# k of batches 1 to 7 transposed by the DMA crossbar instead of TensorE, in a fused two-layer attention and token-mixing kernel

## The chip, the cores and the metric

One NeuronCore of a Trainium2 chip. The metric is device time in microseconds (us) for one execution. Executions of one kernel differ: those of the kernel before took 126.76 to 129.70 us. A run over 1.5% above the fastest of the same kernel is called slow, and ratios use the fast runs alone. "The profile" below is one traced execution; its span runs from the first to the last instruction and is about 1.8 us shorter than the device time.

## The reference, cut to what matters

```python
# q, k, v: [8 batches, 8 heads, 576, 64] float32;  p: [8, 8, 32, 64]
def sm_attn(qq, kk, vv):                       # softmax(q k^T / 8) v
    s = scale * np.matmul(qq, kk.transpose(0, 1, 3, 2)); ...
p_packed = sm_attn(p, k, v)                    # 32 packed rows per head
x = sm_attn(q, p_packed, p_packed)             # back to 576 rows
wq, wk = x @ w_q, x @ w_k                      # token mixing, no softmax
mixed  = (wq @ wk^T / 8) @ x
out    = relu(mixed) @ w_out                   # [8, 576, 512] float32
```

The change concerns the first product only, p against k: in this kernel's matmuls the axis that is summed over lies on the partitions (the rows of on-chip memory), so k has to lie with its 64 head columns on partitions. It arrives with rows on partitions and is transposed: 18 blocks of 128x128 per batch.

## The kernel before

A hand-ordered list names every step; each engine runs its steps strictly in that order. A step `KT.b.c` transposes some of batch b's k blocks on TensorE into PSUM (the memory that TensorE writes), `KE.b.c@V` (or `@A`) copies them to SBUF (the main on-chip memory) on VectorE (or ScalarE), `S1.b.c` multiplies them with p, `X1` takes the exponential. Loads `LD.*` of batches 1 to 7 are issued by GpSimd, stores (inside `OE`) by SyncE (SP).

```python
inpool = ...bufs=4      # k and q as loaded (bf16)      epool = ...bufs=2   # kT and others
opool  = ...bufs=5      # output tiles waiting for their stores
...
def load(x):
    ...
    elif a == "k":
        t = k_in[b] = inpool.tile([P, 2 * C, W], bf16, tag="k_sb", name="k_sb")
        nc.gpsimd.dma_start(t, rows(k, b))          # 576 KB in SBUF, float32 -> bf16 on the way
...
def KT(b, c, eng, bk):                              # 18 blocks in three groups of 8, 8 and 2
    ...
    for n, m in enumerate(ms):
        nc.tensor.transpose(ps[:, n], src[:, m * P:(m + 1) * P], idb if b else idf)
def KE(b, c, eng, bk):
    copy(eng, new("kT", b, [P, NZ, P], pool=epool)[:, z0:z1], T["kt", b, c])
def S1(b, c, eng, bk):                              # scores: needs kT
    ...
    nc.tensor.matmul(ps[...], T["kT", b][:, place(b, m), halves(i)], rhs, start=True, stop=True)
...
def OE(b, t, eng, bk):                              # after every second output tile:
    ...
    for s in range(4):
        nc.sync.dma_start(dst[:, s * 1024:(s + 1) * 1024], o[s * GQ:(s + 1) * GQ]...)
```

A piece of the order, around batch 2:

```
OE.0.2@V WKQ.1.2=0 SET.g2@V OE.0.1@A WE.1.0@V KT.2.1=4 WR.1.0@V WE.1.1@A WR.1.1@V KT.2.2=1
KE.2.1@V GM.1=3 GE.1.1@V LD.q3 GE.1.0@A KT.2.0=5 Y.1=2 KE.2.2@V KE.2.0@V RLR.0@V YE.1@A S1.2.1=7
```

The softmax here doesn't subtract the row's maximum and nothing guards it: scores larger than these inputs give would overflow.

## Time and profile before

| | before |
|---|---|
| device time, median of 2 runs | 128.91 us (128.38 to 129.43) |
| span of the profile, mean granted TensorE clock | 127.6 us, 0.967 |
| TensorE / VectorE / ScalarE busy | 84% / 69% / 62% |
| issue to landing of a k load, median | 19.5 us |

From the page of the kernel before: the span; the busy time of the engines; three rows of 40 equal slices, each digit the busy share in tenths (PEclk: granted clock in tenths); the engines' shares of the chain of work that ended last; and three groups of instructions (engine, operation, output and inputs, shapes, count, busy us, mean ns, idle time before them and who ended it).

```profile
span 127.6 us, 4277 instructions
PE 106.7 (84%) x1794; PEld 71.7 (56%) x1794; DVE 87.9 (69%) x231; ACT 79.0 (62%) x168; POOL 34.6 (27%) x49
...
PE   0299793899998899879999999996999999989800
...
PEclk9999999657999999999999999999999999999997
DMA  3999999399999999999999999999995002664893
...
PE 62%; DVE 11%; ACT 9%; DMA 5%; issue 5%; POOL 3%; SPq 1%; POOLq 0%; ACTq 0%; DVEq 0%
...
L134 ACT ACTIVATE kT<-kT_ps 128x256 bf16<-128x256 bf16 (+2 forms) x8 | 4.8, 595 | 8.7 <-PE kT_ps L286 8.7
...
L138 DVE COPY kT<-kT_ps 128x1024 bf16<-128x1024 bf16 (+1 forms) x15 | 8.8, 606 | 1.2 <-PE kT_ps L286 1.0
L286 PE MATMUL kT_ps<-idb,k_sb 128*128 128x128 bf16 x126 | 9.4, 220 | 0.0
```

TensorE is busy nearly everywhere and holds most of the chain, and the DMA row says 9 tenths until late. The 126 bf16 transposes (L286) overlap one another, so 9.4 us of busy time is an upper bound of what they cost.

The timeline of the kernel before around batch 2 (start, duration, engine, line, operation), cut to SP's stores and to the way of k to the scores:

```profile
38.29 3.83 SPq L521 DMA_DIRECT2D out_dram<-o  x8
...
39.54 0.72 PE L286 MATMUL kT_ps<-idb,k_sb 128*128 128x128 bf16 x10
40.38 0.69 DVE L138 COPY kT<-kT_ps 128x1024 bf16<-128x1024 bf16 x1
...
40.46 0.61 PE L286 MATMUL kT_ps<-idb,k_sb 128*128 128x128 bf16 x8
41.43 0.89 DVE L138 COPY kT<-kT_ps 128x256 bf16<-128x256 bf16 x2
...
41.97 0.44 PE L305 MATMUL e_ps<-pdiag,kT 128*64 128x64 bf16 x16
```

From the first transpose to the first score matmul takes 2.4 us: the transposes hold TensorE for about 1.0 us of it, and the rest is other matmuls and a wait of 0.7 us for ScalarE. SP has issued the last store of this group only at 42.1, when the scores already start.

### The profile page before, as it was taken

What the parts mean: (1) busy time and instruction counts of PE and PEld (TensorE: products, weight loads), DVE (VectorE), ACT (ScalarE), POOL (GpSimd) and SP (SyncE); (2) the same over time, 40 slices, a digit from 0 to 9 for tenths busy, and PEclk for the clock granted to TensorE, in tenths of its full rate; (3) what the DMA queues carried; (4) which work ended last, traced back from release to release, by engine and by line L of the source; (5) the groups of instructions that cost most, each with busy time, mean ns of one, the idle gap of its engine ahead of it and who ended that gap; (6) DMA issues with size and microseconds to landing.
All of it is one profiled execution on the core that took longest, in us unless ns stands there. A gap on an engine that the chain in (4) does not pass through costs nothing.

```text
span 127.6 us, 4277 instructions
## 1 busy us (share of the span) xinstructions
PE 106.7 (84%) x1794; PEld 71.7 (56%) x1794; DVE 87.9 (69%) x231; ACT 79.0 (62%) x168; POOL 34.6 (27%) x49
## 2 busy tenths in 40 slices
PE   0299793899998899879999999996999999989800
PEld 0285382677647447658747764874587765544300
DVE  3028899644996835878998898687785999926310
ACT  4003423962975763977966688785889898578300
POOL 7800211990097000195029004100305006000000
PEclk9999999657999999999999999999999999999997
DMA  3999999399999999999999999999995002664893
GB/s 43 358 201 210 197 206 213 58 161 139 204 212 207 285 285 253 306 255 212 208 208 212 284 283 211 238 309 266 217 251 149 1 5 85 164 167 121 234 285 105
DMA packets 16292, 25.55 MB, mean 200 GB/s; under 512 B 2904, under 2 KB 11096, under 8 KB 16272
## 3 DMA queue, kind: packets, MB, share of 16 engines
q0 software_dynamic: 10720, 14.32, 64.3%
q1 hardware_dynamic: 5552, 10.95, 28.4%
q8 instruction: 14, 0.23, 0.7%
q14 instruction: 6, 0.05, 0.1%
HBM read 30.15 MB, written 9.44 MB: 310 GB/s over the span
## 4 chain that ended last, share of the span: by engine, by line
PE 62%; DVE 11%; ACT 9%; DMA 5%; issue 5%; POOL 3%; SPq 1%; POOLq 0%; ACTq 0%; DVEq 0%
PE out_ps L505 18%; PE kT_ps L286 7%; PE pv_ps L323 5%; PE qT_ps L364 5%; PE aT_ps L415 4%; DMA k<-in_k_dram 3%; PE e_ps L383 3%; POOL a L406 3%; PE e_ps L305 3%; PE mix_ps L475 3%; PE warm_ps L542 2%; DVE rs L395 2%; PE wkq_ps L435 2%; ACT e L311 2%; ACT e L389 2%
## 5 line engine op out<-in xcount | busy, mean ns | idle before, releaser
L505 PE MATMUL out_ps<-wout,relu 128*128 128x512 bf16 x128 | 30.5, 379 | 1.0 <-DVE rec L328 1.0
L406 POOL TENSOR_TENSOR a<-e,rr 128x512 bf16<-128x512 f32 (+1 forms) x15 | 14.0, 947 | 61.5 <-DVE rr L400 39.9
L134 ACT ACTIVATE o<-out_ps 128x512 f32<-128x512 f32 x26 | 15.5, 598 | 8.1 <-PE out_ps L505 7.9
L505 PEld LDWEIGHTS <-relu 128*128 128x128 bf16 x128 | 11.5, 98 | 14.1 <-issue 2.1
L395 DVE TENSOR_REDUCE rs<-e 128x16 f32<-128x512 f32 (+1 forms) x24 | 13.9, 579 | 2.3 <-ACT e L389 2.3
L311 ACT ACTIVATE e<-e_ps 128x512 bf16<-128x512 f32 (+1 forms) x24 | 11.0, 492 | 3.7 <-PE e_ps L305 3.4
L389 ACT ACTIVATE e<-e_ps 128x512 f32<-128x512 f32 (+1 forms) x24 | 12.0, 528 | 1.8 <-PE e_ps L383 1.8
L487 DVE TENSOR_SCALAR relu<-mix_ps 128x512 bf16<-128x512 f32 x17 | 11.0, 683 | 0.0
L364 PE MATMUL qT_ps<-idb,q_sb 128*64 128x128 bf16 x288 | 10.8, 221 | 0.0
L138 DVE COPY qT<-qT_ps 128x1024 bf16<-128x1024 bf16 (+1 forms) x16 | 8.9, 584 | 2.6 <-PE qT_ps L364 2.5
L134 ACT ACTIVATE kT<-kT_ps 128x256 bf16<-128x256 bf16 (+2 forms) x8 | 4.8, 595 | 8.7 <-PE kT_ps L286 8.7
L323 PE MATMUL pv_ps<-v_sb,e 64*64 64x192 bf16 x288 | 9.0, 262 | 0.9 <-ACT e L311 0.9
L138 DVE COPY kT<-kT_ps 128x1024 bf16<-128x1024 bf16 (+1 forms) x15 | 8.8, 606 | 1.2 <-PE kT_ps L286 1.0
L286 PE MATMUL kT_ps<-idb,k_sb 128*128 128x128 bf16 x126 | 9.4, 220 | 0.0
L364 PEld LDWEIGHTS <-q_sb 128*64 128x64 bf16 x288 | 8.6, 110 | 1.1 <-issue 0.4
L305 PE MATMUL e_ps<-pdiag,kT 128*64 128x64 bf16 x288 | 8.2, 203 | 1.1 <-ACT kT L134 0.8
L415 PE MATMUL aT_ps<-idb,a 128*128 128x128 bf16 x80 | 7.9, 231 | 1.3 <-POOL a L406 0.7
L286 PE MATMUL kT_ps<-idf,k 128*128 128x128 f32 x18 | 4.3, 425 | 5.5 <-DMA k<-in_k_dram 5.5
L485 ACT ACTIVATE relu<-mix_ps 128x512 bf16<-128x512 f32 x15 | 8.3, 599 | 0.6 <-PE mix_ps L475 0.5
L305 PEld LDWEIGHTS <-kT 128*64 128x64 bf16 x288 | 6.6, 117 | 3.6 <-issue 1.2
L323 PEld LDWEIGHTS <-e 64*64 64x64 bf16 x288 | 6.4, 113 | 3.4 <-issue 1.3
L138 DVE COPY o<-out_ps 128x512 f32<-128x512 f32 x6 | 4.1, 688 | 5.8 <-PE out_ps L505 5.8
(79 smaller groups left out, 197.7 us busy)
## 6 DMA issues: line engine op xcount, KB each, us to landing
out_dram<-o SPq DMA_DIRECT2D x64, 128.0 KB, 4.2
v_sb<-in_v_dram POOLq DMA_DIRECT2D x8, 576.0 KB, 18.8
q_sb<-in_q_dram POOLq DMA_DIRECT2D x8, 576.0 KB, 17.8
k_sb<-in_k_dram POOLq DMA_DIRECT2D x7, 576.0 KB, 19.5
k<-in_k_dram SPq DMA_DIRECT2D x2, 576.0 KB, 4.8
out_dram<-o_rem SPq DMA_DIRECT2D x4, 256.0 KB, 4.3
wout<-in_moe_w_out_dram POOLq DMA_DIRECT2D x2, 256.0 KB, 4.1
pbf<-in_p_dram POOLq DMA_DIRECT2D x1, 224.0 KB, 11.7
```

Of the source, the lines that this page charges most:

```text
L134: nc.scalar.activation(o, i, COPY)
L138: nc.vector.tensor_copy(o, i)
L286: nc.tensor.transpose(ps[:, n], src[:, m * P:(m + 1) * P], idb if b else idf)
L305: nc.tensor.matmul(ps[halves(i), at[0]:at[1] + 1:at[1] - at[0]], T["kT", b][:, place(b, m), halves(i)], rhs, start=True, stop=True)
L311: nc.scalar.activation(e1[:, 2 * z0:2 * z1], T["s1", b, c], EXP, scale=scale)
L323: nc.tensor.matmul(T["pv", b][i][halves(cc)], lhsT, rhs, start=n == 0, stop=n == R - 1, skip_group_check=True)
L364: nc.tensor.transpose(ps[halves(x), z - z0], q_in[b][:, x, r * Dh:(r + 1) * Dh], idb)
L389: nc.scalar.activation(e2, T["s2", b, c].rearrange("a t i c (x l) -> a (t i c x) l", l=L), EXP, scale=scale)
L395: nc.vector.tensor_reduce(rs, T["e2", (b, c)], axis=AX, op=ADD)
L406: e.tensor_tensor(a2[:, 2 * c:2 * c + n].rearrange("a t i (u l) -> a (t i u) l", l=L), T["e2", (b, c)], T["rr", (b, c)].to_broadcast((P, n ...
L415: nc.tensor.transpose(ps[:, i, t - 2 * c], T["a2", b][:, t, i], idb)
L505: nc.tensor.matmul(ps, lhsT, wout[:, j, :], start=j == 0, stop=j == NJ - 1)
```

## The change

Intent: free TensorE of 126 transposes and VectorE and ScalarE of 21 copies out of PSUM, by one DMA transpose per batch (a crossbar transpose), SBUF to SBUF, issued by SP. Every `KT.b.*` and `KE.b.*` of batches 1 to 7 leaves the order, and one `TR.b` stands where the batch's first `KT` stood:

```diff
-OE.0.2@V WKQ.1.2=0 SET.g2@V OE.0.1@A WE.1.0@V KT.2.1=4 WR.1.0@V WE.1.1@A WR.1.1@V KT.2.2=1
-KE.2.1@V GM.1=3 GE.1.1@V LD.q3 GE.1.0@A KT.2.0=5 Y.1=2 KE.2.2@V KE.2.0@V RLR.0@V YE.1@A S1.2.1=7
+...OE.0.1@A WE.1.0@V TR.2 WR.1.0@V WE.1.1@A WR.1.1@V GM.1=3 GE.1.1@V LD.q3 GE.1.0@A Y.1=2 RLR.0@V
+YE.1@A S1.2.1=7 ...                       (the same for batches 1 and 3 to 7)
@@
     def place(b, m):
-        return sum(KM if b else KM0, []).index(m)
+        return m if b else sum(KM0, []).index(m)
@@
+    def TR(b, eng, bk):
+        kT = new("kT", b, [P, NZ, P], pool=epool)
+        nc.sync.dma_start(kT, k_in[b].rearrange("a u n -> a (u n)"), transpose=True)
```

More of the change, by code (lines that the diff above doesn't have):

```diff
@@ L16 @@
 WC.0@P PP.0.0@V QE.0.2@A PT.0=7 PE.0@A QE.0.1@V PX.1=1 S2.0.1=3 QE.0.0@V WC.1@P PXE.1.0@V S2.0.0=2
-PXE.1.1@V X2.0.1@A S2.0.2=4 X2.0.0@A RS.0.1@V PX.2=0 KT.1.2=5 RR.0.1@V PXE.2.1@A AM.0.1@P QK.0=7
-RS.0.0@V KT.1.0=6 X2.0.2@A KT.1.1=3 RR.0.0@V AM.0.0@P RS.0.2@V KE.1.2@A AT.0.1=1 RR.0.2@V AM.0.2@V
-AT.0.2=2 PXE.2.0@A KE.1.0@A S1.1.2=4 X1.1.2@A LD.O LD.k2 AT.0.0=5 KE.1.1@V AE.0.2@A AE.0.1@V
-S1.1.0=0 QKE.0@A X1.1.0@A S1.1.1=3 WKQ.0.2=6 X1.1.1@A WKQ.0.1=4 WR.0.0@A AE.0.0@V WKQ.0.0=1
-WE.0.1@V PV.1.0=2,5 WR.0.1@V LD.v2 WE.0.0@A SET.g0@V PV.1.1 PV.1.2 RC.1.1@V RC.1.0@V GM.0=7
@@ L22 @@
-PP.1.0@V PP.1.1@V GE.0.0@V QT.1.1=0 GE.0.1@A PT.1=3 Y.0=4 QT.1.0=6 YE.0@V QT.1.2=1 PE.1@V QE.1.1@A
-LD.q2 QE.1.0@V MX.0.0=2,5 MX.0.1=7,4 S2.1.1=3 QE.1.2@A S2.1.2=0 S2.1.0=1 LD.k3 MR.0=6 RL.0.0@A
-RL.0.1@A QK.1=2 RL.0.2@V RL.0.3@V X2.1.2@A X2.1.0@A RS.1.2@V RR.1.2@V RS.1.0@V RR.1.0@V LD.v3
-X2.1.1@A OT.0.3=5 RS.1.1@V OT.0.0=7 OE.0.3@A AM.1.2@P RR.1.1@V AM.1.0@P OT.0.2=0 QKE.1@A AT.1.0=4
-OE.0.0@A AM.1.1@V AT.1.2=1 AE.1.0@A AE.1.2@A AT.1.1=3 OT.0.1=5 WKQ.1.0=2 AE.1.1@A WKQ.1.1=7
-OE.0.2@V WKQ.1.2=0 SET.g2@V OE.0.1@A WE.1.0@V KT.2.1=4 WR.1.0@V WE.1.1@A WR.1.1@V KT.2.2=1
@@ L28 @@
-KE.2.1@V GM.1=3 GE.1.1@V LD.q3 GE.1.0@A KT.2.0=5 Y.1=2 KE.2.2@V KE.2.0@V RLR.0@V YE.1@A S1.2.1=7
-MR.1=0 MX.1.0=4,3 RLR.1@V X1.2.1@A MX.1.1=1,2 S1.2.0=5 OT.1.4=6 RL.1.2@V RL.1.3@A RL.1.0@A
-RL.1.1@V OT.1.0=7 OT.1.1=0 LD.k4 LD.v4 OE.1.4@A OT.1.2=3 OE.1.0@A X1.2.0@A OT.1.3=2 PV.2.0=4,1
-S1.2.2=6 OE.1.2@A LD.q4 OE.1.1@V SET.v3@V OE.1.3@A X1.2.2@A QT.2.2=7 PV.2.1 PV.2.2 QE.2.2@V
-KT.3.2=5 RC.2.1@V QT.2.1=0 QT.2.0=3 RC.2.0@V PP.2.1@V QE.2.0@A PP.2.0@V PT.2=2 QE.2.1@V PE.2@V
-KT.3.0=6 S2.2.2=7 S2.2.1=1 X2.2.2@A KE.3.0@V KE.3.2@V S1.3.0=4 QK.2=0 S1.3.2=2 X2.2.1@A RS.2.2@V
@@ L34 @@
-RS.2.1@V S2.2.0=3 X1.3.0@A X2.2.0@A KT.3.1=7 KE.3.1@A PV.3.0=6,5 RR.2.1@V X1.3.2@A S1.3.1=1 LD.k5
-RR.2.2@V RS.2.0@V QKE.2@A RR.2.0@V AM.2.2@P AM.2.1@P AM.2.0@V LD.v5 AT.2.1=4 X1.3.1@A AT.2.2=3
-AT.2.0=7 PV.3.1 AE.2.0@A AE.2.2@V PV.3.2 AE.2.1@V LD.q5 WKQ.2.2=2 WKQ.2.1=0 WKQ.2.0=1 WR.2.0@A
-RC.3.1@V PP.3.1@V RC.3.0@V QT.3.1=3 WR.2.1@A PP.3.0@V WE.2.0@A QT.3.2=4 WE.2.1@V GM.2=7 QE.3.2@A
-GE.2.1@A QE.3.1@V PT.3=5 QT.3.0=2 PE.3@V GE.2.0@V LD.k6 Y.2=6 S2.3.2=0 S2.3.1=1 KT.4.0=4 KT.4.2=3
-QE.3.0@A YE.2@V X2.3.2@A KE.4.2@A KT.4.1=5 KE.4.0@V LD.v6 MX.2.1=7,6 X2.3.1@A MX.2.0=2,0 S1.4.0=3
@@ L40 @@
-S1.4.2=4 QK.3=1 KE.4.1@V RL.2.0@V LD.q6 S1.4.1=5 S2.3.0=2 RL.2.1@V RL.2.3@A RL.2.2@V X1.4.0@A
-RS.3.1@V X1.4.1@A RR.3.1@V PV.4.0=6,3 X1.4.2@A X2.3.0@A RS.3.2@V RR.3.2@V PV.4.1 PV.4.2 RC.4.0@V
-OT.2.1=7 PP.4.0@V AM.3.2@P OT.2.3=5 OE.2.1@A RS.3.0@V QKE.3@A OE.2.3@A RR.3.0@V OT.2.2=4 AT.3.2=0
-OT.2.0=2 AM.3.1@V RC.4.1@V AM.3.0@P AE.3.2@V WKQ.3.2=7 MR.2=6 OE.2.2@A PP.4.1@V AT.3.1=1 PT.4=5
-AE.3.1@V OE.2.0@A AT.3.0=4 AE.3.0@V KT.5.0=0 WKQ.3.1=3 RLR.2@A PE.4@A LD.k7 WKQ.3.0=2 LD.v7
-QT.4.1=1 WE.3.0@A KE.5.0@V WE.3.1@V WR.3.1@V LD.q7 S1.5.0=6 WR.3.0@A GM.3=5 KT.5.1=4 KT.5.2=0
@@ L46 @@
-QE.4.1@V GE.3.1@A GE.3.0@V KE.5.2@A Y.3=3 X1.5.0@A YE.3@A KE.5.1@V QT.4.0=2 S1.5.2=7 QK.4=1
-X1.5.2@A S1.5.1=5 X1.5.1@A QT.4.2=0 MX.3.1=4,6 QE.4.0@V MX.3.0=3,7 QE.4.2@V PV.5.0=2,0 PV.5.1
-RL.3.3@V PV.5.2 RL.3.2@V RL.3.0@A S2.4.1=5 RL.3.1@A MR.3=6 OT.3.3=3 RC.5.0@V RLR.3@V X2.4.1@A
-QKE.4@V S2.4.0=7 RS.4.1@V OT.3.4=4 S2.4.2=6 OE.3.3@A X2.4.0@A RS.4.0@V OT.3.0=5 RR.4.1@V AM.4.1@P
-OE.3.4@A OT.3.2=1 X2.4.2@A OE.3.0@A RS.4.2@V OT.3.1=3 RR.4.2@V OE.3.2@A RR.4.0@V PP.5.0@V AM.4.2@P
-AM.4.0@V RC.5.1@V AT.4.1=7 AT.4.2=4 AE.4.1@V OE.3.1@A PP.5.1@V AT.4.0=6 KT.6.0=5 AE.4.2@A
@@ L52 @@
-WKQ.4.1=2 WKQ.4.2=1 KE.6.0@V AE.4.0@A WR.4.1@V WKQ.4.0=3 PT.5=7 KT.6.2=4 KT.6.1=0 WR.4.0@V
-WE.4.1@A WE.4.0@A GM.4=6 S1.6.0=5 GE.4.1@A GE.4.0@V QT.5.0=2 Y.4=1 QT.5.2=3 KE.6.1@V QE.5.0@V
-KE.6.2@A X1.6.0@A YE.4@A QE.5.2@V PE.5@A QT.5.1=6 S1.6.2=4 S1.6.1=0 MX.4.1=5,1 X1.6.1@A MX.4.0=2,7
+PXE.1.1@V X2.0.1@A S2.0.2=4 X2.0.0@A RS.0.1@V PX.2=0 TR.1 RR.0.1@V PXE.2.1@A AM.0.1@P QK.0=7
+RS.0.0@V X2.0.2@A RR.0.0@V AM.0.0@P RS.0.2@V AT.0.1=1 RR.0.2@V AM.0.2@V AT.0.2=2 PXE.2.0@A
+S1.1.2=4 X1.1.2@A LD.O LD.k2 AT.0.0=5 AE.0.2@A AE.0.1@V S1.1.0=0 QKE.0@A X1.1.0@A S1.1.1=3
@@ new lines @@
+WKQ.0.2=6 X1.1.1@A WKQ.0.1=4 WR.0.0@A AE.0.0@V WKQ.0.0=1 WE.0.1@V PV.1.0=2,5 WR.0.1@V LD.v2
+WE.0.0@A SET.g0@V PV.1.1 PV.1.2 RC.1.1@V RC.1.0@V GM.0=7 PP.1.0@V PP.1.1@V GE.0.0@V QT.1.1=0
+GE.0.1@A PT.1=3 Y.0=4 QT.1.0=6 YE.0@V QT.1.2=1 PE.1@V QE.1.1@A LD.q2 QE.1.0@V MX.0.0=2,5
+MX.0.1=7,4 S2.1.1=3 QE.1.2@A S2.1.2=0 S2.1.0=1 LD.k3 MR.0=6 RL.0.0@A RL.0.1@A QK.1=2 RL.0.2@V
+RL.0.3@V X2.1.2@A X2.1.0@A RS.1.2@V RR.1.2@V RS.1.0@V RR.1.0@V LD.v3 X2.1.1@A OT.0.3=5 RS.1.1@V
+OT.0.0=7 OE.0.3@A AM.1.2@P RR.1.1@V AM.1.0@P OT.0.2=0 QKE.1@A AT.1.0=4 OE.0.0@A AM.1.1@V AT.1.2=1
@@ new lines @@
+AE.1.0@A AE.1.2@A AT.1.1=3 OT.0.1=5 WKQ.1.0=2 AE.1.1@A WKQ.1.1=7 OE.0.2@V WKQ.1.2=0 SET.g2@V
+OE.0.1@A WE.1.0@V TR.2 WR.1.0@V WE.1.1@A WR.1.1@V GM.1=3 GE.1.1@V LD.q3 GE.1.0@A Y.1=2 RLR.0@V
+YE.1@A S1.2.1=7 MR.1=0 MX.1.0=4,3 RLR.1@V X1.2.1@A MX.1.1=1,2 S1.2.0=5 OT.1.4=6 RL.1.2@V RL.1.3@A
+RL.1.0@A RL.1.1@V OT.1.0=7 OT.1.1=0 LD.k4 LD.v4 OE.1.4@A OT.1.2=3 OE.1.0@A X1.2.0@A OT.1.3=2
+PV.2.0=4,1 S1.2.2=6 OE.1.2@A LD.q4 OE.1.1@V SET.v3@V OE.1.3@A X1.2.2@A QT.2.2=7 PV.2.1 PV.2.2
+QE.2.2@V TR.3 RC.2.1@V QT.2.1=0 QT.2.0=3 RC.2.0@V PP.2.1@V QE.2.0@A PP.2.0@V PT.2=2 QE.2.1@V
@@ new lines @@
+PE.2@V S2.2.2=7 S2.2.1=1 X2.2.2@A S1.3.0=4 QK.2=0 S1.3.2=2 X2.2.1@A RS.2.2@V RS.2.1@V S2.2.0=3
+X1.3.0@A X2.2.0@A PV.3.0=6,5 RR.2.1@V X1.3.2@A S1.3.1=1 LD.k5 RR.2.2@V RS.2.0@V QKE.2@A RR.2.0@V
+AM.2.2@P AM.2.1@P AM.2.0@V LD.v5 AT.2.1=4 X1.3.1@A AT.2.2=3 AT.2.0=7 PV.3.1 AE.2.0@A AE.2.2@V
+PV.3.2 AE.2.1@V LD.q5 WKQ.2.2=2 WKQ.2.1=0 WKQ.2.0=1 WR.2.0@A RC.3.1@V PP.3.1@V RC.3.0@V QT.3.1=3
+WR.2.1@A PP.3.0@V WE.2.0@A QT.3.2=4 WE.2.1@V GM.2=7 QE.3.2@A GE.2.1@A QE.3.1@V PT.3=5 QT.3.0=2
+PE.3@V GE.2.0@V LD.k6 Y.2=6 S2.3.2=0 S2.3.1=1 TR.4 QE.3.0@A YE.2@V X2.3.2@A LD.v6 MX.2.1=7,6
@@ new lines @@
+X2.3.1@A MX.2.0=2,0 S1.4.0=3 S1.4.2=4 QK.3=1 RL.2.0@V LD.q6 S1.4.1=5 S2.3.0=2 RL.2.1@V RL.2.3@A
+RL.2.2@V X1.4.0@A RS.3.1@V X1.4.1@A RR.3.1@V PV.4.0=6,3 X1.4.2@A X2.3.0@A RS.3.2@V RR.3.2@V PV.4.1
+PV.4.2 RC.4.0@V OT.2.1=7 PP.4.0@V AM.3.2@P OT.2.3=5 OE.2.1@A RS.3.0@V QKE.3@A OE.2.3@A RR.3.0@V
+OT.2.2=4 AT.3.2=0 OT.2.0=2 AM.3.1@V RC.4.1@V AM.3.0@P AE.3.2@V WKQ.3.2=7 MR.2=6 OE.2.2@A PP.4.1@V
+AT.3.1=1 PT.4=5 AE.3.1@V OE.2.0@A AT.3.0=4 AE.3.0@V TR.5 WKQ.3.1=3 RLR.2@A PE.4@A LD.k7 WKQ.3.0=2
+LD.v7 QT.4.1=1 WE.3.0@A WE.3.1@V WR.3.1@V LD.q7 S1.5.0=6 WR.3.0@A GM.3=5 QE.4.1@V GE.3.1@A
@@ new lines @@
+GE.3.0@V Y.3=3 X1.5.0@A YE.3@A QT.4.0=2 S1.5.2=7 QK.4=1 X1.5.2@A S1.5.1=5 X1.5.1@A QT.4.2=0
+MX.3.1=4,6 QE.4.0@V MX.3.0=3,7 QE.4.2@V PV.5.0=2,0 PV.5.1 RL.3.3@V PV.5.2 RL.3.2@V RL.3.0@A
+S2.4.1=5 RL.3.1@A MR.3=6 OT.3.3=3 RC.5.0@V RLR.3@V X2.4.1@A QKE.4@V S2.4.0=7 RS.4.1@V OT.3.4=4
+S2.4.2=6 OE.3.3@A X2.4.0@A RS.4.0@V OT.3.0=5 RR.4.1@V AM.4.1@P OE.3.4@A OT.3.2=1 X2.4.2@A OE.3.0@A
+RS.4.2@V OT.3.1=3 RR.4.2@V OE.3.2@A RR.4.0@V PP.5.0@V AM.4.2@P AM.4.0@V RC.5.1@V AT.4.1=7 AT.4.2=4
+AE.4.1@V OE.3.1@A PP.5.1@V AT.4.0=6 TR.6 AE.4.2@A WKQ.4.1=2 WKQ.4.2=1 AE.4.0@A WR.4.1@V WKQ.4.0=3
@@ L55 @@
+PT.5=7 WR.4.0@V WE.4.1@A WE.4.0@A GM.4=6 S1.6.0=5 GE.4.1@A GE.4.0@V QT.5.0=2 Y.4=1 QT.5.2=3
+QE.5.0@V X1.6.0@A YE.4@A QE.5.2@V PE.5@A QT.5.1=6 S1.6.2=4 S1.6.1=0 MX.4.1=5,1 X1.6.1@A MX.4.0=2,7
 X1.6.2@A QE.5.1@V RL.4.1@A PV.6.0=3,6 PV.6.1 RL.4.0@A PV.6.2 RL.4.3@V RL.4.2@V RC.6.1@V PP.6.1@V
@@ L58 @@
 QT.6.1=5 AT.5.0=1 RS.5.2@V PP.6.0@V RR.5.2@V AM.5.2@V AM.5.1@P QKE.5@A QE.6.2@A QE.6.1@V AT.5.2=7
-AT.5.1=2 PT.6=3 KT.7.2=6 KT.7.0=4 PE.6@V AE.5.2@A S2.6.1=0 AE.5.1@V AE.5.0@A KE.7.0@V S2.6.2=5
-WKQ.5.2=7 KE.7.2@V KT.7.1=3 WKQ.5.0=1 X2.6.2@A WR.5.1@A X2.6.1@A WKQ.5.1=2 WR.5.0@A RS.6.2@V
-WE.5.0@A S1.7.2=4 WE.5.1@A S1.7.0=5 QK.6=6 KE.7.1@V X1.7.0@A RS.6.1@V RR.6.2@V RR.6.1@V S1.7.1=0
-AM.6.1@P X1.7.1@A X1.7.2@A QT.6.0=7 GM.5=3 PV.7.0=1,2 PV.7.1 GE.5.1@A GE.5.0@V PV.7.2 QE.6.0@V
-RC.7.1@V Y.5=5 MR.4=0 S2.6.0=4 AM.6.2@P YE.5@V QKE.6@A AT.6.1=3 RC.7.0@V PP.7.0@V AT.6.2=6 RLR.4@A
@@ L64 @@
-AE.6.1@A PP.7.1@V AE.6.2@V X2.6.0@A MX.5.1=7,5 MX.5.0=0,1 MR.5=2 RL.5.3@V PT.7=6 RL.5.0@A
-WKQ.6.1=3 RLR.5@A PE.7@V WKQ.6.2=4 RL.5.2@V QK.7=5 RS.6.0@V RL.5.1@A QT.7.1=6 QT.7.0=0 RR.6.0@V
-QT.7.2=2 OT.5.0=1 QE.7.1@A WE.6.1@A WR.6.1@A AM.6.0@V S2.7.1=7 QE.7.0@V OE.5.0@A QE.7.2@V AT.6.0=6
-QKE.7@V S2.7.0=3 X2.7.1@A AE.6.0@V X2.7.0@A OT.5.4=0 WR.6.0@A OE.5.4@A RS.7.1@V RR.7.1@V RS.7.0@V
-WKQ.6.0=2 RR.7.0@V S2.7.2=1 WE.6.0@A OT.5.2=5 GM.6=6 OT.5.3=7 X2.7.2@A AM.7.1@P RS.7.2@V GE.6.1@V
-AM.7.0@P GE.6.0@V RR.7.2@V Y.6=3 AT.7.1=4 OE.5.2@A OE.5.3@A AM.7.2@V YE.6@V AE.7.1@V AT.7.0=0
@@ L70 @@
-AE.7.0@A AT.7.2=2 MX.6.1=1,5 AE.7.2@V MX.6.0=6,3 OT.5.1=7 RL.6.3@A WKQ.7.2=4 RL.6.1@V RL.6.2@V
-WKQ.7.1=2 OE.5.1@V WR.7.1@V WKQ.7.0=0 RL.6.0@A WR.7.0@A WE.7.1@A OT.6.1=5 WE.7.0@A MR.6=1 GM.7=6
-OE.6.1@A GE.7.1@A GE.7.0@V OT.6.2=3 Y.7=7 OE.6.2@A YE.7@V OT.6.3=4 MR.7=2 RLR.6@A OE.6.3@V RLR.7@A
-MX.7.0=0,5 MX.7.1=6,7 RL.7.3@A RL.7.1@V RL.7.2@A OT.6.0=3 RL.7.0@V OT.7.4=1 OT.7.0=2 OE.6.0@A
-OT.7.1=4 OE.7.4@A OT.7.3=7 OT.7.2=6 OE.7.0@A OE.7.1@V OE.7.2@V OE.7.3@A
+AT.5.1=2 PT.6=3 TR.7 PE.6@V AE.5.2@A S2.6.1=0 AE.5.1@V AE.5.0@A S2.6.2=5 WKQ.5.2=7 WKQ.5.0=1
@@ new lines @@
+X2.6.2@A WR.5.1@A X2.6.1@A WKQ.5.1=2 WR.5.0@A RS.6.2@V WE.5.0@A S1.7.2=4 WE.5.1@A S1.7.0=5 QK.6=6
+X1.7.0@A RS.6.1@V RR.6.2@V RR.6.1@V S1.7.1=0 AM.6.1@P X1.7.1@A X1.7.2@A QT.6.0=7 GM.5=3 PV.7.0=1,2
+PV.7.1 GE.5.1@A GE.5.0@V PV.7.2 QE.6.0@V RC.7.1@V Y.5=5 MR.4=0 S2.6.0=4 AM.6.2@P YE.5@V QKE.6@A
+AT.6.1=3 RC.7.0@V PP.7.0@V AT.6.2=6 RLR.4@A AE.6.1@A PP.7.1@V AE.6.2@V X2.6.0@A MX.5.1=7,5
+MX.5.0=0,1 MR.5=2 RL.5.3@V PT.7=6 RL.5.0@A WKQ.6.1=3 RLR.5@A PE.7@V WKQ.6.2=4 RL.5.2@V QK.7=5
+RS.6.0@V RL.5.1@A QT.7.1=6 QT.7.0=0 RR.6.0@V QT.7.2=2 OT.5.0=1 QE.7.1@A WE.6.1@A WR.6.1@A AM.6.0@V
@@ new lines @@
+S2.7.1=7 QE.7.0@V OE.5.0@A QE.7.2@V AT.6.0=6 QKE.7@V S2.7.0=3 X2.7.1@A AE.6.0@V X2.7.0@A OT.5.4=0
+WR.6.0@A OE.5.4@A RS.7.1@V RR.7.1@V RS.7.0@V WKQ.6.0=2 RR.7.0@V S2.7.2=1 WE.6.0@A OT.5.2=5 GM.6=6
+OT.5.3=7 X2.7.2@A AM.7.1@P RS.7.2@V GE.6.1@V AM.7.0@P GE.6.0@V RR.7.2@V Y.6=3 AT.7.1=4 OE.5.2@A
+OE.5.3@A AM.7.2@V YE.6@V AE.7.1@V AT.7.0=0 AE.7.0@A AT.7.2=2 MX.6.1=1,5 AE.7.2@V MX.6.0=6,3
+OT.5.1=7 RL.6.3@A WKQ.7.2=4 RL.6.1@V RL.6.2@V WKQ.7.1=2 OE.5.1@V WR.7.1@V WKQ.7.0=0 RL.6.0@A
+WR.7.0@A WE.7.1@A OT.6.1=5 WE.7.0@A MR.6=1 GM.7=6 OE.6.1@A GE.7.1@A GE.7.0@V OT.6.2=3 Y.7=7
@@ L75 @@
+OE.6.2@A YE.7@V OT.6.3=4 MR.7=2 RLR.6@A OE.6.3@V RLR.7@A MX.7.0=0,5 MX.7.1=6,7 RL.7.3@A RL.7.1@V
+RL.7.2@A OT.6.0=3 RL.7.0@V OT.7.4=1 OT.7.0=2 OE.6.0@A OT.7.1=4 OE.7.4@A OT.7.3=7 OT.7.2=6 OE.7.0@A
+OE.7.1@V OE.7.2@V OE.7.3@A
 """
@@ L524 @@
     done = {}
-    steps = dict(PX=PX, PXE=PXE, WC=WC, KT=KT, KE=KE, S1=S1, X1=X1, PV=PV, RC=RC, PP=PP,
+    steps = dict(PX=PX, PXE=PXE, WC=WC, TR=TR, KT=KT, KE=KE, S1=S1, X1=X1, PV=PV, RC=RC, PP=PP,
                  PT=PT, PE=PE, QK=QK, QKE=QKE, QT=QT, QE=QE, S2=S2, X2=X2, RS=RS, RR=RR, AM=AM,
```

## The prediction

> **What bounds the kernel now.** TensorE and the DMA engines share it. The page: PE busy 84% of 127.6 us, DVE 69%, ACT 62%; the chain that ended last is 62% PE. The DMA row of the page reads 9 tenths from 10 to 97 us, and loads land late: in the issue-to-landing times the median for a batch of k is 19.5 us. k of batches 1 to 7 lands at 18, 33, 43, 57, 66, 77, 89 us (estimated from issue and landing), and its TensorE transposes start at 22, 40, 49, 60, 68, 81, 93 (timeline): only 2 to 7 us of slack.
>
> **Removed.** 126 transposes of 219 ns, pipelined to 1.0 us per batch (chain of waits: x18 in 1.00 us), and 21 PSUM copies (0.28 to 0.69 us on DVE, up to 1.0 on ACT; about 11 us of the two engines). On the chain, the bf16 transposes are about 4.3 us of PE and the DVE copies about 1.5: a gain of at most about 6 us.
>
> **Added.** Seven crossbar transposes of 576 KB on the SP queue[...]. The trace before has none. Estimate: the Trainium skill, "DMA: Bandwidth & Descriptors", § Latency and other measured facts, gives 261 GB/s for a DMA transpose: 2.3 us of all 16 engines each, 16 us in all, on engines that are already full. To that comes descriptor issue on SP, and the round trip: a 128 KB store on the same queue lands 5 to 6 us after issue while the loads run (2 us once they are done). I estimate 8 us (5 to 12) from issue to landing.
>
> **Moved: the step that decides.** SP issues in order, and most transposes stand behind the stores of an earlier batch, just before their use. From the times of before, the last store ahead of the transpose is issued at 42.1, 52.2, 71.1, 84.1, 96.3 us for batches 2, 3, 5, 6, 7; the score matmuls that need the result start at 42.0, 52.1, 70.1, 83.0, 95.6. So the transpose starts when its result is wanted, and TensorE, also in order, waits out its whole latency. Batch 4 (right behind batch 3's, wanted 9 us later) is nearly free; batch 1 (k lands at 18, wanted at 25) loses 0 to 2 us. Five waits of about 8 us are 40; some 7 are absorbed where the chain runs over DVE, ACT and POOL just there (52 to 56, 68 to 72, 94 to 99 us); 6 to 7 are saved. Sum: about +27 us.
>
> **Prediction.** 155 us, 80% range 138 to 176. Faster by over 2%: 0.03; within 2%: 0.03; slower by over 2%: 0.94.
>
> **What would show it.**
> - Right: the list of waits has PE (or its weight loads) at the score matmuls waiting for a DMA kT<-k_sb, five long waits of 5 to 12 us, sum 25 to 50; PE busy falls by 7 us or more in sum and below 70% of the span; the transposes' issue comes directly behind the stores on SP, long after k has landed.
> - DMA row still 9 tenths while loads run; loads end later than 97 us; issue to landing of a transpose 5 to 12 us.
> - Wrong: waits at the score matmuls under 2 us each, or the time lost elsewhere (copies out of PSUM waiting for store buffers, loads that come too late).
>
> **What would make it wrong.** A transpose that lands in 3 to 4 us gives about 135; one much slower (small descriptors, long issue on SP, also delaying the stores behind it) 180 or more. If the loads fall behind through the added traffic, waits appear at q and v also.

## The result

190.6 us (190.26 to 190.95, 2 runs) against 128.91 us: 1.49 times as long (95% interval 1.463 to 1.519), outside the predicted range of 138 to 176. A ratio here is the mean time of one kernel's fast runs over that of the other's of the same rounds, so it is not quite the ratio of the medians quoted.

From the page of the changed kernel, the parts shown of before; in place of the groups of copies there is the group of the score matmuls:

```profile
span 189.2 us, 4018 instructions
PE 111.8 (59%) x1668; PEld 72.6 (38%) x1668; DVE 80.2 (42%) x216; ACT 76.5 (40%) x162; POOL 34.6 (18%) x49
...
PE   0898309993000099359996000898159908999960
...
PEclk9999955999555559965899655569858965999997
DMA  5999999999999904999997999004830490016595
...
DMA 42%; PE 36%; DVE 6%; SPq 5%; ACT 3%; POOL 3%; issue 2%; POOLq 0%; DVEq 0%; ACTq 0%
...
L307 PE MATMUL e_ps<-pdiag,kT 128*64 128x64 bf16 x288 | 10.5, 232 | 55.2 <-DMA kT<-k_sb 55.2
```

The last line is the main reading: TensorE stood 55.2 us in front of the score matmuls, waiting for transposes. The zeros in the PE row are these waits. Two things are less expected. TensorE is busy for *longer* (111.8 us, before 106.7) although 126 instructions are gone, and after the waits the granted clock is half (the 5s in PEclk; a slice that is partly at half clock shows 6 to 8).

The timeline of the changed kernel at batch 2, then at batch 6 (in brackets the idle time before and its releaser):

```profile
41.66 3.75 SPq L523 DMA_DIRECT2D out_dram<-o  x8
46.74 12.16 SPq L281 DMA_TRANSPOSE kT<-k_sb  x1
...
65.98 0.64 PE L307 MATMUL e_ps<-pdiag,kT 128*64 128x64 bf16 x16 [21.01 <-DMA kT<-k_sb]
...
130.71 4.27 SPq L523 DMA_DIRECT2D out_dram<-o  x7
135.09 2.07 SPq L281 DMA_TRANSPOSE kT<-k_sb  x1
...
139.15 0.64 PE L307 MATMUL e_ps<-pdiag,kT 128*64 128x64 bf16 x16 [5.40 <-DMA kT<-k_sb]
```

k of batch 2 had been in SBUF since 33.4 us; SP, in order, came to the transpose at 46.7 behind the stores; TensorE had arrived at the scores at 45.0. The same transpose, same size, held SP for 12.2 us at batch 2 and for 2.1 us at batch 6. The table has all seven, worked out from issue and landing times in the trace; "loads beside it" is what the trace's packet records show of load bytes (as written) between issue and landing. (Stores run beside five of them too: 784 and 744 KB at batches 2 and 5, 236 to 304 KB at batches 3, 6 and 7.)

| batch | k landed | TensorE at the scores | transpose issued | landed | issue to landing | TensorE waited | loads beside it |
|---|---|---|---|---|---|---|---|
| 1 | 18.4 | 25.2 | 18.4 | 28.4 | 10.1 | 3.2 | 1424 KB |
| 2 | 33.4 | 45.0 | 46.7 | 65.9 | 19.2 | 21.0 | 2380 KB |
| 3 | 42.4 | 77.8 | 77.0 | 82.3 | 5.3 | 4.6 | 0 |
| 4 | 54.1 | after landing | 80.3 | 86.7 | 6.4 | 0 | 325 KB |
| 5 | 65.2 | 102.4 | 104.1 | 118.1 | 14.0 | 15.7 | 1526 KB |
| 6 | 95.7 | 133.8 | 135.1 | 139.1 | 4.0 | 5.4 | 0 |
| 7 | 109.1 | 151.7 | 151.9 | 156.9 | 5.0 | 5.2 | 0 |

The step of the prediction that was to decide holds: for batches 2, 3, 5, 6 and 7 the transpose is issued between 0.8 us before and 1.8 us after its result is wanted, so TensorE waits out the latency. What was mis-sized there is the latency, which is not one number: 4.0 to 5.3 us without loads beside it, 6.4 us beside 325 KB of them, 10 to 19 us beside 1.4 MB and more.

Engine activity of the changed kernel in four stretches: the first two are the 5 and 8 us after the two longest waits, at half clock; the other two are the waits of batches 2 and 6. The columns are the stretch, its length, busy us (and instructions) of TensorE, its weight loads, VectorE, ScalarE and GpSimd, granted clock, DMA share, GB/s. (A DMA share above 1 means that packets overlap on the engines.)

```profile
66.00:71.20 5.20, 5.20 (x45) 2.29 (x46) 1.73 (x3) 2.28 (x4) 0.00 (x0) 0.50 0.01 3
...
118.10:125.80 7.70, 7.01 (x123) 5.29 (x124) 2.72 (x6) 3.29 (x8) 0.00 (x0) 0.50 0.01 2
...
46.74:65.94 19.20, 0.00 (x0) 0.00 (x0) 0.00 (x0) 0.00 (x0) 0.00 (x0) 0.51 1.14 200
...
135.09:139.11 4.02, 0.00 (x0) 0.00 (x0) 0.00 (x0) 0.00 (x0) 0.00 (x0) 0.62 0.91 207
```

In these two waits, and in that of batch 5, no engine does anything once the transpose is issued: the others have run dry behind TensorE. (In batch 7's wait VectorE, ScalarE and GpSimd still work 1.0 to 1.6 us.) The DMA engines moved nearly the same in both, 200 and 207 GB/s; what differs is how much was under way, 3.8 MB against 0.8 MB with the stores. And right after the long waits the DMA engines do nothing (share 0.01): GpSimd, whose queue holds the next loads behind work that depends on TensorE (its longest wait was 35.7 us), was stopped as well, so the loads that the wait had let through are not followed by others.

### The profile page after: what moved, and what is told of

It reads as the page before. It is cut to its first block, busy times and chain, and to the rows that moved or that the text cites. A ratio compares the mean times of both kernels' runs of the same rounds, so it can differ in the third digit from the quotient of the medians.

```text
span 189.2 us, 4018 instructions
## 1 busy us (share of the span) xinstructions
PE 111.8 (59%) x1668; PEld 72.6 (38%) x1668; DVE 80.2 (42%) x216; ACT 76.5 (40%) x162; POOL 34.6 (18%) x49
## 3 DMA queue, kind: packets, MB, share of 16 engines
q1 hardware_dynamic: 21904, 15.08, 34.7%
## 4 chain that ended last, share of the span: by engine, by line
DMA 42%; PE 36%; DVE 6%; SPq 5%; ACT 3%; POOL 3%; issue 2%; POOLq 0%; DVEq 0%; ACTq 0%
DMA kT<-k_sb 30%; PE out_ps L507 12%; DMA k_sb<-in_k_dram 8%; SPq L523 5%; PE e_ps L307 4%; PE qT_ps L366 4%; PE pv_ps L325 4%; DMA out_dram<-o 4%; PE mix_ps L477 2%; PE e_ps L385 2%; PE aT_ps L417 2%; POOL a L408 1%; PE g_ps L453 1%; PE wkq_ps L437 1%; ACT aT L131 1%
## 5 line engine op out<-in xcount | busy, mean ns | idle before, releaser
L307 PE MATMUL e_ps<-pdiag,kT 128*64 128x64 bf16 x288 | 10.5, 232 | 55.2 <-DMA kT<-k_sb 55.2
L307 PEld LDWEIGHTS <-kT 128*64 128x64 bf16 x288 | 9.0, 144 | 58.7 <-DMA kT<-k_sb 56.3
L397 DVE TENSOR_REDUCE rs<-e 128x16 f32<-128x512 f32 (+1 forms) x24 | 13.9, 578 | 9.4 <-ACT e L391 9.3
L135 DVE CAST g_sb<-g_ps 64x128 bf16<-64x128 f32 x9 | 2.5, 283 | 27.3 <-ACT g_sb L131 26.9
L366 PE MATMUL qT_ps<-idb,q_sb 128*64 128x128 bf16 x288 | 13.2, 250 | 0.0
L366 PEld LDWEIGHTS <-q_sb 128*64 128x64 bf16 x288 | 10.7, 129 | 1.6 <-issue 1.2
L489 DVE TENSOR_SCALAR rem<-mr_ps 128x256 bf16<-128x256 f32 x3 | 1.3, 446 | 22.8 <-PE mr_ps L482 22.8
L325 PE MATMUL pv_ps<-v_sb,e 64*64 64x192 bf16 x288 | 10.2, 291 | 0.9 <-ACT e L313 0.9
L131 ACT ACTIVATE g_sb<-g_ps 64x128 bf16<-64x128 f32 x7 | 1.9, 272 | 21.4 <-PE g_ps L453 18.3
L437 PE MATMUL wkq_ps<-aT,pqk 128*128 128x256 bf16 (+1 forms) x48 | 8.4, 273 | 0.0
L385 PE MATMUL e_ps<-ppT,qT 128*128 128x64 bf16 x160 | 7.6, 198 | 1.0 <-DVE ppT L135 0.9
## 6 DMA issues: line engine op xcount, KB each, us to landing
v_sb<-in_v_dram POOLq DMA_DIRECT2D x8, 576.0 KB, 13.9
q_sb<-in_q_dram POOLq DMA_DIRECT2D x8, 576.0 KB, 13.9
```

The costliest lines, as they stand in the source:

```text
L131: nc.scalar.activation(o, i, COPY)
L135: nc.vector.tensor_copy(o, i)
L307: nc.tensor.matmul(ps[halves(i), at[0]:at[1] + 1:at[1] - at[0]], T["kT", b][:, place(b, m), halves(i)], rhs, start=True, stop=True)
L325: nc.tensor.matmul(T["pv", b][i][halves(cc)], lhsT, rhs, start=n == 0, stop=n == R - 1, skip_group_check=True)
L366: nc.tensor.transpose(ps[halves(x), z - z0], q_in[b][:, x, r * Dh:(r + 1) * Dh], idb)
L385: nc.tensor.matmul(ps[:, t - 2 * c, i, cc], lhsT, T["ppT", b][:, i, cc], start=True, stop=True)
```

## The experiments

Theory A: TensorE waits out transposes that are issued when they are wanted. Rival B: the transposes' traffic, and the SP time they take, cost it by themselves. Theory C: the lowered clock adds a part. Theory D: an engine alternates packet by packet between loads and transposes, hence 19 us. The runs e1 to e4, e5 to e8 and e9 to e12: each group shares its runs of the kernel before, medians 127.72, 127.50 and 127.14 us. Medians and ranges below are of all runs, ratios of the fast ones. The profiles of e1, e3, e4, e7, e8 and e12 are of slow runs.

### e1: the transposes added, nobody reads them

```diff
 (kernel before, TensorE's transposes kept)
+    def TR(b, eng, bk):
+        kT = new("kTd", b, [P, NZ, P], pool=epool)
+        nc.sync.dma_start(kT, k_in[b].rearrange("a u n -> a (u n)"), transpose=True)
+ TR.1 ... TR.7 in the order, each before the first KT of its batch
```

> The kernel before, with TensorE's transposes as they were, plus the seven crossbar transposes at the changed kernel's places in the SP queue, into a tile that nobody reads. Theory A (TensorE waits out the latency of transposes that start when they are wanted): nobody waits, so most of the 62 us loss goes; 129 to 137 us. Rival B (the added traffic and the SP queue time themselves cost it: loads and stores fall behind): most of the loss stays, 150 us or more.

146.1 us (144.61 to 147.14), ratio 1.139 (1.126 to 1.151). Between the two expectations: over two thirds of the loss goes when nobody waits, but about 18 us stay. The list of waits of e1 for GpSimd shows a new one:

```profile
POOL k_sb L183 <- DMA kTd<-k_sb: 33.4, 2, 19.6
```

GpSimd waited 33.4 us, in two pieces, for k buffers that slow transposes (26.5 and 21.3 us from issue to landing for batches 2 and 3) were still reading; loads and the multiplies that normalise the second softmax stood behind it in the queue.

### e2: no transposes at all for batches 1 to 7

```diff
     def TR(b, eng, bk):
-        kT = new("kT", b, [P, NZ, P], pool=epool)
-        nc.sync.dma_start(kT, k_in[b].rearrange(...), transpose=True)
+        T["kT", b] = T["kT", 0]
```

> Wrong result on purpose: the changed kernel without the crossbar transposes; batches 1 to 7 read batch 0's transposed k. It measures what taking the transposes off TensorE and the copies off VectorE and ScalarE is worth alone. My prediction's term was 6 to 7 us: 122 to 123 us. If the loads bound the kernel now, the gain is under 3 us.

127.51 us (126.35 to 129.0); ratio 0.989 (0.978 to 0.999). The profile's span is 124.7 us. It used batch 0's k everywhere, and the result still passed the comparison, which therefore does not test k sharply. All that the change could save in this order is about 1.4 us (0.1 to 2.8), not the 6 to 7 of the prediction. TensorE is busy 6.3 us less (100.4 us) and only 1.4 us come of it, so its work was not the limit microsecond for microsecond; what the loads are worth is tested in e11.

### e4: TensorE kept busy during the waits

```diff
+    FILL = {2: 85, 3: 15, 5: 65, 6: 19, 7: 19}
     def S1(b, c, eng, bk):
         ps = T["s1", b, c] = bank(...)
+        for _ in range(FILL.pop(b, 0) * 512 // n):      # n: columns of ps
+            nc.tensor.matmul(ps..., warm[:, 0:P], warm[:, 0:n], start=True, stop=True)
```

> The changed kernel with TensorE kept busy in five of its waits by matmuls whose result is overwritten (85, 15, 65, 19, 19 of 512 columns, each bunch shorter than the wait it stands in). In the changed kernel some 29 us of work after the waits ran at a granted clock of one half. Theory C (part of the loss is the lowered clock after the waits): 178 to 184 us and fewer stretches at half clock. Rival (the waits alone are the loss): 190 us whatever the clock does.

186.84 us median, fast runs 183.30 and 185.95; ratio 1.444 (1.422 to 1.465) against 1.491 for the changed kernel, so about 6 us less, though the intervals overlap slightly. The clock row of e4:

```profile
PEclk9999965999999956999999999569999999999995
```

The clock is granted fully in nearly all slices (mean 0.934 against 0.787). In this profile 14.5 us of waiting remain and the fillers take 44.8 us; the rest is 186.0 - 14.5 - 44.8 = 126.7 us. In the changed kernel the rest is 189.2 - 55.2 = 134.0 us. The difference, 7 us, agrees with the 6 us of the timed runs, and TensorE without the fillers is busy 148.8 - 44.8 = 104.0 us in place of 111.8. Theory C is supported, as a small part.

### e10 and e11: the transposes and the kernel before, with few loads

```diff
 (both: the changed kernel and the kernel before)
         elif a == "v":
+            if b: return                  # batches 1 to 7 reuse batch 0's v
...
+            if b: q_in[b] = q_in[0]; return
...
-        vt = v_bufs[b % NL]
+        vt = v_bufs[0]
```

> Wrong data on purpose: the changed kernel without the loads of q and v for batches 1 to 7 (they reuse batch 0's), so that transposes meet few loads. If contention with the loads is what makes them land after 10 to 19 us: each lands 4 to 7 us after issue, the waits at the score matmuls sum to 20 to 30 us, and the time is 20 to 32 us over the same cut of the kernel before (next run): 145 to 155 us. If transposes are slow in themselves: 14 us and more stay.

> Wrong data on purpose: the kernel before without the loads of q and v for batches 1 to 7. The yardstick for the run before this one, and a test of whether the loads bound the kernel before: they do if it falls below 124 us; 125 to 128 us if they don't.

e11, the yardstick: 126.24 us, ratio 0.994 (0.988 to 1.001). With 14 of 21 loads gone the kernel before gains under 1%: loads did not bound it. e10: 168.47 us (166.72 to 168.88), ratio 1.321 (1.312 to 1.330), both results wrong. The first line is of e10's list of waits; the second, of its view of the tile kT, gives issue to landing of the seven transposes:

```profile
PE e_ps L312 <- DMA kT<-k_sb: 34.5, 5, 9.9
...
DMA to landing us min/median/max: 4.0/5.7/8.2
```

No transpose takes over 8.2 us, where the changed kernel's range is 4.0 to 19.2. So contention with loads made the long latencies. It is worth about (190.6 - 128.9) - (168.5 - 126.2) = 19 us of the 62. But the other 42 us stay, more than the 20 to 32 that I expected (and 168 us is outside my 145 to 155): the five latencies still sum to 29.7 us, SP's late arrival adds 4.5 us net (most at batch 2, issued at 43.2 with TensorE waiting since 40.3), which makes the waits 34.5 us, and the mean clock is 0.83.

### e12, e3 and e7: the same transposes issued earlier

```diff
 e3 and e12: in the order, TR.2 directly after LD.k2; TR.3, TR.4, TR.6, TR.7 after the last
 store of batch 0, 1, 2, 3; TR.5 before the first store of batch 2    (e12: with the cut of e10)
 e7: LD.k(b+1) where LD.k(b) stood; kT with bufs=4; k of batches 5 and 6 in the space of batch 0's
 float32 k; TR.2 after LD.k3, TR.3 before and TR.4 after batch 0's stores, TR.5 after batch 1's,
 TR.6 before and TR.7 after batch 2's
```

> Wrong data on purpose: the cut of the two runs before this, with the transposes one group of stores earlier on SP. With landing after 4 to 7 us and some 10 us of lead, the latency should be hidden: waits under 8 us in sum, and within 4 us of the same cut of the kernel before. If it stays 15 us or more above, the loss has another cause than exposed latency.

> The changed kernel with each crossbar transpose put one group of stores earlier on SP, so that it is issued about when its k has landed. Theory A: most of the waits of 5 to 21 us shrink to what the latency of 10 to 19 us under the loads exceeds the 4 to 9 us between landing and use; 140 to 155 us, still slower than before. Rival B (traffic): stays near 185 to 190.

> The changed kernel with k loaded one batch ahead of v and q, four buffers for the transposed k in place of two, no k buffer reused before its transpose is old, and each transpose issued as soon as its k lands. Theory A (exposed latency is most of the loss): the waits at the score matmuls fall below 10 us in sum and the time to 132 to 142 us. If the traffic itself is dear, it stays at 146 us or more even with few waits. In no case under 126, as the kernel with no transposes at all took 127.5.

With few loads, lead is nearly enough: e12 takes 133.81 us (131.70 to 134.72). Its ratio is 1.042 (1.032 to 1.052) against 0.994 for e11, about 6 us over it, where e10 was about 42 over it. Its waits at the scores sum to:

```profile
PE e_ps L311 <- DMA kT<-k_sb: 4.9, 2, 2.8
```

That settles exposed latency as the main cause in this cut: only the places of the transposes differ between e10 and e12. I had expected to come within 4 us of e11; the rest was not pursued. With all loads, lead helps only in part: e3 takes 169.57 us (164.82 to 171.89; only the fastest counts as fast, so there is no ratio), outside my 140 to 155. Its profile has 40.1 us of such waits:

```profile
PE e_ps L306 <- DMA kT<-k_sb: 40.1, 5, 12.7
```

There, batch 2's transpose is issued at 35.0, right after its k landed, but lands at 59.0; and as each DMA on SP waits for the eighth before it, the eighth store behind it goes out at 59.03 only, so that the transpose of batch 3, behind that store, starts at 59.9. e7 failed: outside my 132 to 142, its runs were 161.60, 165.81, 188.73 and 191.03 us, so no single figure stands for it (only the fastest counts as fast). Its profile (164.0 us) has 34.7 us of waits at the scores and transposes that take up to 32.4 us. By that profile, loading k ahead only puts the transposes among the loads. What makes two of its runs 25 us slower stays open.

### e6: loads with packets half as long

```diff
-            nc.gpsimd.dma_start(t, rows(k, b))                 # and the same for v
+            for h in range(2):
+                nc.gpsimd.dma_start(t[:, :, h * W // 2:(h + 1) * W // 2],
+                                    rows(k, b)[:, :, h * W // 2:(h + 1) * W // 2])
```

> The changed kernel with each load of k and v as two DMAs of half rows: packets of 576 bytes in place of 1152, same bytes. In the changed kernel a transpose is 2304 packets of 256 bytes (144 per DMA engine); alone it lands 4 to 5 us after issue, beside loads 14 and 19 us. Theory D (each engine takes one packet from each queue in turn, so that a transpose waits for one load packet per packet of its own): with packets half as long the transposes of batches 2 and 5 land after 9 to 14 us. Rival (the two queues share bytes or time): 19 and 14 us as before, or longer.

One run, of unknown state: 195.78 us. The transposes of batches 2 and 5 land 20.1 and 16.6 us after issue: Theory D falls. At batch 2, 3143 load packets pass beside the transpose (1826 in the changed kernel) but 2200 KB (2380 KB): bytes of load fit, their number does not. In both kernels these transposes land within 1.6 us of the last load then under way. How an engine shares itself between the two queues is not settled beyond this.

### e5 and e9: unread transposes that hold no k buffer

```diff
 (e1, with:)
+    still = const.tile([P, NZ * P], bf16)                # zeros, written once
-        kT = new("kTd", b, [P, NZ, P], pool=epool)
-        nc.sync.dma_start(kT, k_in[b]..., transpose=True)
+        kT = epool.tile([P, NZ, P], bf16, tag="kTd", name="kTd", bufs=1)
+        nc.sync.dma_start(kT, still, transpose=True)
 (e9: and TR.4 to TR.7 after the last store of batch 2, 3, 4, 5)
```

> As the run with unread transposes, but the seven transposes read a constant tile of the same shape, so that no k buffer waits for them. In the run with unread transposes (146.1 us against 127.7) GpSimd stood 33.4 us in two waits for a k buffer that a transpose was still reading, with the next loads and the normalising multiplies behind it in its queue. If those late releases were most of the 18 us: 129 to 136 us. If the added DMA traffic was: 140 us or more.

> As the run whose unread transposes read a constant tile (145.7 us), but never two transposes in a row on SP: the fourth to seventh stand one group of stores later each. There ScalarE stood 13.2 us waiting for a store to free its buffer, while SP was held 30 us by two transposes. If queues held up by transposes are what the unread ones cost: 129 to 137 us. If the DMA engines' time itself is: 141 us or more.

e5: 145.69 us, ratio 1.139. e9: 144.80 us, ratio 1.134 (1.125 to 1.143). Freeing GpSimd brought nothing, for another queue stopped instead. The first line is of e5's waits, the second of e9's; both are ScalarE, which had to wait for a store before it could reuse an output buffer:

```profile
ACT o L134 <- DMA out_dram<-o: 15.0, 3, 13.1
...
ACT o L134 <- DMA out_dram<-o: 9.3, 2, 8.7
```

In e5 two transposes in a row held SP from 71.8 to 101.8 us, with the stores behind them (13 us of that were of my making: the single destination buffer made the second wait for the first). In e9 there is no such pair, the wait for buffers fell by 6 us and the time by 1 only; the last load lands at 104.0, before at 95.3. So of the 18 us that unread transposes cost, waits for k buffers and for stores are seen, and later loads are seen, but these runs do not divide it among them. (By the terms written before e9, over 141 us would mean DMA time; but the runs removed one wait and met another, so that is not shown.) Rival B is thus real. I do not add it to the waits as a separate sum, since in the changed kernel the queues stand still in TensorE's waits anyway; that is an argument, which no run tests.

### e8: batch 7 alone

```diff
 (kernel before; KT.7.*, KE.7.* removed; LD.k7 directly after LD.k6; TR.7 after the last store of batch 3)
```

> The kernel before with batch 7's k alone transposed by the DMA, k of batch 7 loaded ahead of v and q of batch 6, and the transpose issued one group of stores early, near the end of the loads. Only a seventh of the work moves, worth at most 1 us; exposed latency should be small: 126 to 130 us, the same as before. Over 131 us would mean that even one transpose beside loads is exposed.

134.64 us (133.49 to 135.53), ratio 1.052 (1.040 to 1.064): a miss. This one transpose took 16.4 us from issue to landing, across the end of the loads, and exposed:

```profile
PE e_ps L308 <- DMA kT<-k_sb: 5.5, 1, 5.5
```

No version that beats the kernel before was found; issuing the transposes from another queue than SP's was not tried. e2 shows why there is little to look for: with the transposes free of charge the kernel gains 1.1%.

## Why the prediction was wrong

The direction and the mechanism (exposed latency) were right, the size was not: +27 us predicted, +61.6 us in the spans. No single term carries the error. The sum, term by term:

| term of the prediction | predicted | measured | shown by |
|---|---|---|---|
| waits at the score matmuls, batches 2, 3, 5, 6, 7 | 5 x 8 = 40 | 52.0 | table of the result |
| wait of batch 1 | 0 to 2 | 3.2 | the same |
| absorbed by other engines' parts of the chain | -7 | none to be seen | TensorE's idle time outside the waits |
| saved on TensorE, VectorE, ScalarE | -6 to -7 | -0.9 | remainder, 126.7 - 127.6 us; e2 has -1.4 |
| lowered clock after the waits | not thought of | about +7 | e4 |
| sum | +27 | +61.6 | 55.2 + 7.3 - 0.9 |

1. **"I estimate 8 us (5 to 12) from issue to landing."** This step failed: 19.2 and 14.0 us beside loads, 4.0 to 5.3 us without. The five latencies sum to 47.5 us instead of 40; that this is not further off is luck, since two were 17 us longer together than I estimated and three 10 us shorter. SP's late arrival adds 4.2 us net. e10 shows that the loads are the reason for the long ones. It shows too that this step is not all: there the latencies are 4.0 to 8.2 us and the waits sum to 34.5 us, less than my 40, and the kernel is still 42 us over its yardstick, not 27. The next two points and the clock make that up. The 2.3 us of data time, taken from the Trainium skill ("DMA: Bandwidth & Descriptors", § Latency and other measured facts, 261 GB/s), was right where nothing was loaded: at batch 6 the 2304 packets of 256 bytes run from 1.27 to 3.55 us after issue, 589,824 bytes in 2.28 us, or 259 GB/s. The error was to treat a transfer on engines that are already full as its own data time plus a fixed allowance.
2. **"Some 7 are absorbed."** Not so: TensorE's idle time outside these waits was 189.2 - 111.8 - 55.2 = 22.2 us, and all its idle time before was 127.6 - 106.7 = 20.9 us, so the waits came on top of the old gaps. The likely reason: the chain's turns over VectorE, ScalarE and GpSimd need TensorE's results too, so a stopped TensorE does not let them catch up by more than what was already under way.
3. **"6 to 7 are saved."** I added the pieces of the chain that belong to the removed instructions. e2 shows that without them only about 1.4 us go: other work takes their place.
4. **"TensorE and the DMA engines share it."** Removing the transposes and their copies (e2) gives 1.1%, removing two thirds of the loads (e11) 0.6%, which is not clear of zero. Busy rows near 9 tenths on both did not mean that relief of either one would help. My reading, which no run isolates: the order interleaves four engines so tightly that relief of one is taken up by the next.
5. **"PE busy falls by 7 us or more in sum."** It rose by 5.1, through the half clock (104.0 us in e4, where the clock was granted). The Trainium skill ("TensorE: Matmul & The Clock Gate", § Why this matters for your kernels) advises against idle gaps over about 3 us between bursts of matmuls. This trace agrees: after the waits of 4.6 to 21.0 us the granted clock was 0.50 for 3 to 9 us of work. I had not read the page for what *waiting* would do.
6. **What held.** The transposes are issued directly behind the stores, long after k has landed (batch 1's excepted); they are wanted at that moment; batch 4 is free; the waits are named at the score matmuls (two of the five inside the 5 to 12 us, their sum of 52 just over the 25 to 50); PE busy is below 70% of the span (59%); the DMA row is at 9 tenths while loads run; loads end later (the last at 116.5 us).

The loss of 62 us, taken apart: 55 us of waits and 7 us of half clock, less 1 us saved. Of it, some 19 us go when the loads go (e10 against e11), and about 36 of the other 42 us, in that cut, when the transposes also start earlier (e12).

## What to carry to other kernels

Moving work from an engine to a DMA trades an in-order step of a few hundred nanoseconds for a latency, so move its *start* as well: look at which queue issues it, what stands before it there, and how long before its use it can be issued; here a transfer placed where the old instruction stood was issued when its result was already wanted. Measure the latency in the stage where it will run, beside the same traffic, not alone. Before either, delete the work (wrong result allowed) and time that: here one such run would have shown a ceiling of about 1%.

## What the Trainium skill lacked or had wrong

- "Advanced Engine Details and Errata", § X-Bar Transpose (TRN2), says that transpose DMAs are as fast as regular ones. The runs do not contradict it: without loads 4.0 us for 576 KB, where the kernel's first regular load of 576 KB landed after 4.3 us; beside loads 10 to 19 us, where the 576 KB loads of the same kernel took 13.0 to 13.9 us in the median. What no page read gives is a transpose's latency beside loads (up to 32.4 us in e7).
- No page read says how long issuing a transpose holds the issuing queue while the DMA engines are busy: SP was taken for 2.1 us without loads and for 12.2 us beside them (up to 18.2 us in e7), against 0.4 us for a store. Everything behind it on SP is late by that.
- "DMA: Bandwidth & Descriptors", § Queues, rings and completion order, says that an engine takes turns between queues packet by packet, with several descriptors to a packet. e6 (load descriptors half as long, 20.1 us after 19.2, one run) does not speak against turns of bundles, but does against turns of single descriptors; how long a transpose then takes is not to be had from the page.
- "VectorE: DVE Perf Modes", § Rules for kernel authors, advises TensorE for a 128x128 transpose where PSUM will do. 18 blocks took 1.0 us of TensorE, pipelined, against 4.0 us and more by DMA.
- "TensorE: Matmul & The Clock Gate", § Why this matters for your kernels, names idle gaps over about 3 us. In the kernel before a shorter one, of 2.1 us (19.8 to 21.9 us), was followed from 23.5 us on by 6.8 us at a clock of 0.5; in e11, where the longest gap of that stretch was 0.9 us, the clock stayed at 1.0.
